# Third stage of a retention and multiplicative-FFN kernel: VectorE's block transposes behind the first work item, v and natural k on ScalarE's DMA queue, unit 10 transposed by TensorE

## The chip, the cores and the metric

The kernel runs on one core of one Trainium2 chip. The metric is the device time of one execution in microseconds (us). The kernel before took 881.2 us, the median of three runs (878.97, 881.2, 881.26); the profiled execution took 879.61, of which the profile's span is 877.6.

Short names used below: PE is TensorE's matmuls, PEld its weight loads, DVE VectorE, ACT ScalarE, POOL GpSimd, and SP SyncE, whose queue issues most of the DMAs. L448 is line 448 of the kernel.

## The reference

The program has two parts. Retention comes first: for 8 sequences, 8 heads, 576 positions and 64 features a head, every score of a query against an earlier key is scaled by a power of a decay, without a softmax, and multiplied with v. The result, 4608 tokens of 512 features, then goes through a multiplicative feed-forward network.

```python
scores = scale * np.matmul(q, k.transpose(0, 1, 3, 2))          # (8, 8, 576, 576)
gamma = 1.0 - 2.0 ** (-5.0 - np.arange(H, dtype=np.float32))
Dmat = np.where(rel >= 0, gamma[:, None, None] ** rel[None], 0.0)
x = np.matmul(scores * Dmat, v)                                 # then to (4608, 512)
a = x @ w1                                                      # (4608, 1024)
b = x @ w2
h = a * b @ w3
return h @ w_out                                                # (4608, 512)
```

The four weight matrices come as 64-bit floats. All else is 32-bit.

## The kernel before

**Units.** The sequences are taken in four pairs i = 0 to 3. The positions of a pair are cut into five chunks c: a short one of 64 positions first, then four of 128. A unit is g = 5i + c, so there are 20 units, and units 5, 10 and 15 are the short first units of the second, third and fourth pair. The decay is split into a factor on q and one on v, so only the triangle of the mask is left inside a chunk.

**The attention work of a unit.**
- `load` (L103) brings q, k or v in natural form, positions on the partitions: one DMA each, 512 KB (256 KB for a short unit).
- `scale` (L203) multiplies q and v by their decay factors on GpSimd.
- `front` (L215) transposes k and q on TensorE, so that the features lie on the partitions, and ScalarE copies them out of PSUM as kT and qT.
- `score` (L232): 32 TensorE matmuls of kT and qT (tile sc, L241), and VectorE multiplies with the triangular mask into pm (L244).
- `state` (L248): k^T v of the chunk is added on TensorE to a running state (L263), and ScalarE copies it to sb for the next unit. The last chunk of a pair has none. It needs k and v in natural form.
- `pv` (L270): TensorE multiplies sb with qT (L291, where there is a chunk before) and pm with v (L298); ScalarE copies the sum into the token tile xT (L303).

**The block form.** For units from 10 on, k and q reach kT and qT without TensorE. `load_blocks` (L168) loads 32x32 blocks with many small DMAs of 32 KB: 16 for k and 16 for q of a full unit, 8 and 8 for a short one, all issued by SyncE. `scale_blocks` (L183) multiplies the blocks of q by the decay in two GpSimd instructions. `front_blocks` (L193) has VectorE transpose every block in one instruction for k and one for q (L198). The natural k is still loaded, for `state`. Tiles of blocks share two buffers with the natural q (tag ld_q), so the loads of one unit wait until the transposes of the unit before have read theirs.

**The feed-forward network.** 192 positions of both sequences of a pair make a token group (i, n), 12 in all. `up(i, n, fp)` (L476) computes a quarter of the products x w1 and x w2 with Strassen's seven products: TensorE multiplies (L493), ScalarE copies the first product (L506, later L513), VectorE adds the others up (L498) and multiplies both halves (L519). `down(x, y)` (L583) does the same for two groups of 128 tokens against the product of w3 and w_out (L599 on TensorE, L603 on VectorE, L621 and L627 on ScalarE) and SyncE stores the result (L644). `carry` is one ScalarE copy (L551). The sums of tokens that Strassen's form needs are made on GpSimd (L467). Seven PSUM buffers (pool acc) serve all of it in rotation.

**The order.** The program is scheduled by hand: each engine does its instructions in the order in which they are written. Three stages follow each other: weights and the first pair, the product of w3 and w_out, and then the third stage, the loop at L805 over the steps g = 5 to 19. There the list `todo` holds the work items, and `work(n)` takes the next n of them. A step does items, then pv(g), then state and score of g + 1, then further items. In steps 10 to 19 there are two items ahead of pv. For the steps that matter, as the code gives them:

| step g | item 1 | item 2 | behind score of g + 1 |
|---|---|---|---|
| 8 | up(1,0,0) | none | none |
| 9 | up(1,0,1) | none | none |
| 10 | up(1,0,2) | up(1,0,3) | up(1,1,0), a down |
| 11 | up(1,1,1) | a down | up(1,1,2) |
| 12 | up(1,1,3) | up(1,2,0) | carry |
| 13 | a down | up(1,2,1) | up(1,2,2) |
| 14 | up(1,2,3) | up(2,0,0) | a down |
| 15 | up(2,0,1) | a down | up(2,0,2), up(2,0,3) |
| 16 | up(2,1,0) | carry | a down, up(2,1,1) |
| 17 | up(2,1,2) | up(2,1,3) | up(2,2,0), a down |
| 18 | up(2,2,1) | a down | up(2,2,2), up(2,2,3) |

Before, the code of a step with blocks (L814 to L829) puts scale_blocks behind item 1 and front_blocks behind item 2, and behind pv(g) SyncE's queue gets the natural v and k of unit g + 2, then its k blocks, then its q blocks.

Of the kernel before, what the change touches and what calls it, by code (L numbers as in the profile page):

```python
# [38 lines left out]
def kernel(  # L39
# [13 lines left out]
    nc = tc.nc  # L53
# [11 lines left out]
    NC = (S + P - 1) // P  # L65
# [3 lines left out]
    G = NB2 * NC  # L69
# [33 lines left out]
    def load(g, names, engine=nc.sync):  # L103
        i, c = divmod(g, NC)
        sz = sizes[c]
        src = {"k": k, "q": q, "v": v}
        for nm in names:
            t = pools["ld"].tile([P, 2 * H, D], F32, tag="ld_" + nm, name="ld_" + nm)
            engine.dma_start(
                t[:sz], src[nm][2 * i:2 * i + 2, :, starts[c]:starts[c] + sz, :].rearrange("b h p d -> p (b h) d"))  # L110
            live[nm, g] = t
# [56 lines left out]
    def load_blocks(g, nm):  # L168

        i, c = divmod(g, NC)  # L170
        n = sizes[c] // BL
        t = pools["ld"].tile([P, 2 * NP, P // BL, BL], F32, tag="ld_q", name="bl_" + nm)
        src = {"k": k, "q": q}[nm][2 * i:2 * i + 2].rearrange("b (p a) s d -> a (b p) s d", a=2)
        for a in range(2):
            for f in range(D // BL):
                part = (a * (D // BL) + f) * BL
                for m in range(n):
                    s0 = starts[c] + m * BL
                    nc.sync.dma_start(t[part:part + BL, :, m, :],  # L179
                                      src[a, :, s0:s0 + BL, f * BL:(f + 1) * BL].rearrange("m r x -> r m x"))  # L180
        live["bl_" + nm, g] = t

    def scale_blocks(g):  # L183
        c = g % NC
        n, n0 = sizes[c] // BL, starts[c] // BL
        t = live["bl_q", g]
        for b in range(2):
            part = t[:, b * NP:(b + 1) * NP, :n, :]
            nc.gpsimd.tensor_tensor(
                out=part, in0=part, in1=gqs[:, :, n0:n0 + n].unsqueeze(3).to_broadcast([P, NP, n, BL]),  # L190
                op=ALU.mult)

    def front_blocks(g):  # L193
        c = g % NC
        n = sizes[c] // BL
        for nm in "kq":
            dst = pools["fr"].tile([P, 2, NP, P], F32, tag=nm + "T", name=nm + "T", bufs=1 if nm == "k" else 2)
            nc.vector.transpose(  # L198
                dst[:, :, :, :sizes[c]].rearrange("p b m (n x) -> p (b m) n x", x=BL),
                live["bl_" + nm, g][:, :, :n, :])  # L200
            live[nm + "T", g] = dst

    def scale(g, nm, scalar=False):  # L203
        c = g % NC
        sz = sizes[c]
        t, gam = live[nm, g], {"q": gq, "v": gk}[nm]
        t = t[:sz].rearrange("p (b h) d -> p b h d", b=2)
        if scalar:
            for h in range(H):
                nc.scalar.mul(t[:, :, h, :], t[:, :, h, :], gam[:sz, c, h:h + 1])  # L210
            return
        nc.gpsimd.tensor_tensor(  # L212
            out=t, in0=t, in1=gam[:sz, c].unsqueeze(1).unsqueeze(3).to_broadcast([sz, 2, H, D]), op=ALU.mult)

    def front(g, names="kq"):  # L215
        c = g % NC
        sz = sizes[c]
        for nm in names:
            src = live[nm, g]
            dst = pools["fr"].tile([P, 2, NP, P], F32, tag=nm + "T", name=nm + "T",  # L220
                                   bufs=1 if nm == "k" and g >= NC else 2)
            for b in range(2):
                tp = acc.tile([P, NP, P], F32, tag="acc", name="tp")
                for p in range(NP):
                    h = b * H + 2 * p
                    nc.tensor.transpose(tp[:, p, :sz],  # L226
                                        src[:sz, h:h + 2, :].rearrange("p a d -> p (a d)"),
                                        ident[:sz, :sz])
                nc.scalar.copy(dst[:, b, :, :sz], tp[:, :, :sz])
            live[nm + "T", g] = dst  # L230
# [39 lines left out]
    def pv(g):  # L270
        i, c = divmod(g, NC)
        sz = sizes[c]
        live["x", g] = True
        qT, vs, pm = live["qT", g], live["v", g], live["pm", g]

        parts = []
        for n in range(NB):
            lo, hi = max(starts[c], n * TB), min(starts[c] + sz, (n + 1) * TB)
            if lo < hi:
                m = i * NB + n  # L280
                if ("xT", m) not in live:
                    live["xT", m] = xps[m % 4 == 3].tile([P, NP, 2, TB], F32, tag="xT", name="xT")
                parts.append((live["xT", m], lo - n * TB, lo - starts[c], hi - lo))

        banks = [acc.tile([P, 2, 2, P], F32, tag="acc", name="xps") for r in range(2)]
        order = [(b, n) for b in range(2) for n in range(2)]
        if c > 0:
            for m, (b, n) in enumerate(order):
                for r, j in ((0, 0), (0, 1), (1, 0), (1, 1)):
                    p = 2 * r + n  # L290
                    nc.tensor.matmul(banks[r][heads[j ^ r], b, n, :sz], live["sb", g][heads[j], b, p, :],  # L291
                                     qT[heads[j], b, p, :sz], start=(m == 0), stop=False,
                                     skip_group_check=True)
        for m, (b, n) in enumerate(order):
            for r in range(2):
                for half in range(2):
                    p, j = 2 * r + n, half ^ r
                    nc.tensor.matmul(banks[r][heads[half], b, n, :sz], vs[:sz, b * H + 2 * p + j, :],  # L298
                                     pm[:sz, b, j, p, :sz], start=(c == 0 and m == 0), stop=True,
                                     skip_group_check=True)  # L300
        for x, to, fr, n in parts:
            for r in range(2):
                nc.scalar.copy(  # L303
                    x[:, 2 * r:2 * r + 2, :, to:to + n].rearrange("p n b s -> p b n s"),
                    banks[r][:, :, :, fr:fr + n])
# [272 lines left out]
    def ahead(x, y, n=3):  # L578
        todo_sums = pair_of(x, y)[2]
        for _ in range(min(n, len(todo_sums))):  # L580
            aside.append(todo_sums.pop(0))
# [203 lines left out]
    def work(n):  # L785
        for _ in range(min(n, len(todo))):
            fn, *args = todo.pop(0)

            nxt = next((x for x in todo if x[0] is not carry), None)
            if nxt and nxt[0] is down and fn is not carry:  # L790
                if fn is down:
                    args.append(nxt[1:])
                else:
                    last = args == [*every[max(nxt[1][0], nxt[2][0])], NQ - 1]
                    ahead(*nxt[1:], 1 if last else 3)
            fn(*args)
# [4 lines left out]
    state(NC)  # L801
    score(NC)
    scale(NC + 1, "q")
    in_blocks = [u >= 2 * NC for u in range(G)] + [False] * 2
    for g in range(NC, G):  # L805
        c = g % NC
        n = -(-len(todo) // (NC - c))
        if g + 2 < G and not in_blocks[g + 2]:
            load(g + 2, "kq")
        if g + 1 < G:  # L810
            scale(g + 1, "v")
            if not in_blocks[g + 1]:
                front(g + 1)
        half = (n + 1) // 2  # L814
        if in_blocks[g + 1]:
            work(1)
            scale_blocks(g + 1)
            work(1)
            front_blocks(g + 1)
            half = max(half - 2, 0)  # L820
        work(half)
        pv(g)
        if g + 2 < G:
            load(g + 2, "v")
        if in_blocks[g + 2]:
            if (g + 2) % NC != NC - 1:
                load(g + 2, "k")
            load_blocks(g + 2, "k")
            load_blocks(g + 2, "q")  # L829
        if g + 1 < G:  # L830
            state(g + 1)
            score(g + 1)
        if g + 2 < G and not in_blocks[g + 2]:
            scale(g + 2, "q")
        if g == NC + 1:
            strassen_tokens(1, 0)
            todo.extend((up, 1, 0, fp) for fp in range(2))
        work(n // 2)
        if c == NC - 1:
            add_pair(g // NC)  # L840
# [44 lines left out]
```

## Time and profile before

| engine | busy us | share of the span |
|---|---|---|
| TensorE, weight loads | 777.6 | 89% |
| GpSimd | 112.2 | 13% |
| DMA from HBM | 53.03 MB | 71 GB/s with the stores |

How to read the rows shown later: in the timeline a row has its start and length in us, the engine, the line, the operation and its tiles (out<-in), then in brackets how long the engine stood idle ahead of it and what ended that wait. In the chain of waits the program is followed back from its end, at each step to what released it. A row of waits gives the total us, how many times, and the longest. Ends of matmuls are modelled, so a wait of a tenth of a us means little.

Some durations in the third stage, as the timeline and the chain have them: an up takes TensorE 9.10 us (9.30 just behind a score), a down 12.09, pv 1.03 and 1.90, a state 0.93, a score of a full unit 1.99. A full k transpose on VectorE takes 1.24 us. GpSimd's scaling of a natural v or q takes 1.90, of a unit's q blocks 2.06. SyncE is held 0.45 us (median) by the issue of one block DMA, which lands about 2 us after it.

### The profile page before, as it was taken

The numbers are of one execution on the slowest core, as the hardware profiler recorded it, in microseconds if no ns is written. First come the engines' busy times: TensorE is split into PE (matmuls) and PEld (weight loads), VectorE is DVE, ScalarE is ACT, GpSimd is POOL, SyncE is SP. The second block draws the span as 40 slices with busy tenths as digits, with TensorE's granted clock in tenths as the row PEclk, the third lists the DMA queues.
The fourth block names the chain that finished last, engine by engine and source line by source line (L and its number), as shares of the span: only waits on it lengthen the run. The fifth ranks groups of instructions, "written<-read, shape, count | busy, mean of one in ns | idle before, by whom it ended". The sixth has DMA issues, their size and how long they took to land.

```text
span 877.6 us, 15316 instructions
## 1 busy us (share of the span) xinstructions
PE 851.1 (97%) x6357; PEld 777.6 (89%) x6357; DVE 458.7 (52%) x783; ACT 193.7 (22%) x386; POOL 112.2 (13%) x92
## 2 busy tenths in 40 slices
PE   5899999999999999899999999999999999999998
PEld 4799999554888999799989998989999999999996
DVE  5999998972544334544444534444534424434243
ACT  3676334553122211101111101110101101001000
POOL 3000020003003201301203012203020101000000
PEclk9999999999999999899999999999999999999999
DMA  9993443427045335513244053251310000000001
GB/s 199 217 229 91 98 121 97 144 96 108 0 100 123 92 49 89 99 32 79 43 70 76 4 105 93 41 88 34 65 33 25 2 24 1 24 25 1 25 1 49
DMA packets 190644, 63.46 MB, mean 72 GB/s; under 512 B 178792, under 2 KB 178792, under 8 KB 190576
## 3 DMA queue, kind: packets, MB, share of 16 engines
q1 hardware_dynamic: 188912, 62.19, 33.5%
q8 instruction: 50, 0.82, 0.4%
q10 hardware_dynamic: 1664, 0.30, 0.3%
q14 instruction: 18, 0.15, 0.1%
HBM read 53.03 MB, written 9.44 MB: 71 GB/s over the span
## 4 chain that ended last, share of the span: by engine, by line
PE 85%; DVE 5%; SPq 2%; issue 2%; DMA 0%; ACT 0%; DVEq 0%; POOL 0%; POOLq 0%; ACTq 0%
PE up L493 44%; PE po L599 24%; PE ps L448 6%; PE sc L241 4%; PE xps L298 3%; SPq L179 2%; PE tp L226 1%; PE xps L291 1%; DVE c L498 1%; PE st L263 1%; DVE qT L198 1%; PE tp L438 1%; DVE kT L198 1%; DVE e L383 0%; DMA bl_q<-in_q_dram 0%
## 5 line engine op out<-in xcount | busy, mean ns | idle before, releaser
L498 DVE TENSOR_TENSOR c<-up,c 128x384 f32<-128x384 f32 x240 | 133.5, 556 | 209.8 <-PE up L493 204.4
L493 PE MATMUL up<-xT,wA 128*128 128x192 f32 x1152 | 213.1, 328 | 0.5 <-ACT xT L303 0.5
L493 PEld LDWEIGHTS up<-xT,wA 128*128 128x128 f32 x1152 | 191.7, 191 | 3.4 <-issue 1.0
L493 PE MATMUL up<-T,wS 128*128 128x192 f32 x768 | 140.6, 326 | 2.1 <-DVE T L467 2.1
L493 PEld LDWEIGHTS up<-T,wS 128*128 128x128 f32 x768 | 127.4, 190 | 2.4 <-issue 2.4
L599 PE MATMUL po<-w3o,ab 128*128 128x256 f32 x456 | 104.2, 380 | 0.2 <-ACT ot L621 0.2
L599 PEld LDWEIGHTS po<-w3o,ab 128*128 128x128 f32 x456 | 85.9, 190 | 12.2 <-ACT ot L621 0.6
L603 DVE TENSOR_TENSOR ot<-po,ot 128x256 f32<-128x256 f32 x90 | 38.2, 424 | 73.5 <-PE po L599 72.9
L513 ACT COPY c<-up 128x384 f32<-128x384 f32 x48 | 22.9, 478 | 226.4 <-PE up L493 222.2
L493 PE MATMUL up<-xT,wS 128*128 128x192 f32 x384 | 70.6, 327 | 0.6 <-DVE c L498 0.5
L493 PE MATMUL up<-T,wA 128*128 128x192 f32 x384 | 70.2, 326 | 0.0
L599 PE MATMUL po<-wB,forms 128*128 128x256 f32 x288 | 65.1, 379 | 0.0
L493 PEld LDWEIGHTS up<-xT,wS 128*128 128x128 f32 x384 | 63.6, 190 | 1.5 <-DVE c L498 1.5
L493 PEld LDWEIGHTS up<-T,wA 128*128 128x128 f32 x384 | 63.7, 190 | 0.0
L244 DVE TENSOR_TENSOR pm<-sc,mask 128x512 f32<-128x512 f32 (+1 forms) x80 | 45.5, 628 | 33.0 <-PE sc L241 33.0
L599 PEld LDWEIGHTS po<-wB,forms 128*128 128x128 f32 x288 | 54.7, 190 | 7.4
L448 PE MATMUL ps<-wo,w3T 128*128 128x512 f32 x128 | 56.4, 593 | 0.2 <-ACT w3T L440 0.2
L212 POOL TENSOR_TENSOR ld_v<-ld_v,gk 128x1024 f32<-128x1024 f32 (+1 forms) x17 | 32.7, 1926 | 155.9 <-DMA ld_v<-in_v_dram 142.9
L506 ACT COPY c<-up 128x384 f32<-128x384 f32 x48 | 22.9, 477 | 132.7 <-PE up L493 84.0
L519 DVE TENSOR_TENSOR ab<-c 128x768 f32<-128x768 f32 x48 | 46.4, 967 | 3.8
L448 PEld LDWEIGHTS ps<-wo,w3T 128*128 128x128 f32 x128 | 23.7, 190 | 27.3 <-issue 26.8
L241 PE MATMUL sc<-qT,kT 64*128 64x128 f32 (+1 forms) x640 | 40.6, 280 | 6.4 <-DVE qT L198 6.4
(75 smaller groups left out, 795.7 us busy)
## 6 DMA issues: line engine op xcount, KB each, us to landing
raw<-in_moe_w_dram SPq DMA_DIRECT2D x24, 512.0 KB, 3.6
ld_v<-in_v_dram SPq DMA_DIRECT2D x16, 512.0 KB, 5.0
ld_k<-in_k_dram SPq DMA_DIRECT2D x14, 512.0 KB, 6.9
out_dram<-ot SPq DMA_DIRECT2D x24, 256.0 KB, 2.0
bl_k<-in_k_dram SPq DMA_DIRECT2D x144, 32.0 KB, 2.2
bl_q<-in_q_dram SPq DMA_DIRECT2D x144, 32.0 KB, 2.0
raw<-in_moe_w_dram SPq DMA_DIRECT2D x16, 256.0 KB, 6.7
ld_q<-in_q_dram SPq DMA_DIRECT2D x8, 512.0 KB, 8.4
```

Source lines behind the costliest of these rows:

```text
L212: nc.gpsimd.tensor_tensor(out=t, in0=t, in1=gam[:sz, c].unsqueeze(1).unsqueeze(3).to_broadcast([sz, 2, H, D]), op=ALU.mult)
L241: nc.tensor.matmul(sc[j][:sz, p, :sz], kT[hs, b, p, :sz], qT[hs, b, p, :sz], start=True, stop=True)
L244: nc.vector.tensor_mul(pm[:sz, b, j, :, :sz], sc[j][:sz, :, :sz], mask[:sz, :sz].unsqueeze(1).to_broadcast([sz, NP, sz]))
L298: nc.tensor.matmul(banks[r][heads[half], b, n, :sz], vs[:sz, b * H + 2 * p + j, :], pm[:sz, b, j, p, :sz], start=(c == 0 and m == 0), stop ...
L448: nc.tensor.matmul(ps, live["w3T", ft][:, g, :], live["wo"][:, g, :], start=(g == 0), stop=(g == KF - 1))
L493: nc.tensor.matmul(ps[:, w, :], a[:, w, r, :], b[:, r, :], start=(new and w == r == 0), stop=(w == r == 1), skip_group_check=True)
L498: nc.vector.tensor_add(c[:, to], ps, c[:, sb])
L506: nc.scalar.copy(c[:, 0], p1)
L513: nc.scalar.copy(c[:, 0], p1)
L519: nc.vector.tensor_mul(ab[:, 4 * fp:4 * fp + 4, :], c[:, :, 0, :], c[:, :, 1, :])
L599: nc.tensor.matmul(ps[nm], a[A][:, f, :], live["W"][B][:, f, :], start=(f == 0 and not on), stop=(f == NP - 1), skip_group_check=True)
L603: nc.vector.tensor_add(ot[:, to[0], to[1]], ps[nm], ot[:, sb[0], sb[1]])
```

## The change

Four things change in the loop of the third stage; the order of the work items stays.

- The transposes of unit g + 1 come behind item 1, not item 2, and the scaling of its q blocks comes ahead of item 1. This is to have kT and qT ready well before score asks for them.
- The block loads of unit g + 2 are issued directly behind those transposes, q before k, and not behind pv(g).
- The natural v and k of a unit in block form are issued from ScalarE's queue, so that SyncE's queue holds only blocks and stores. Their place behind pv(g) stays.
- Unit 10, the short first unit of the third pair, is no longer in block form: its k and q are loaded naturally in step 8, and TensorE transposes them in step 9 (the comparison `u > 2 * NC`). So SyncE can issue unit 11's blocks a step earlier in the run.

```diff
-    in_blocks = [u >= 2 * NC for u in range(G)] + [False] * 2
+    in_blocks = [u > 2 * NC for u in range(G)] + [False] * 2
     for g in range(NC, G):
         c = g % NC
         n = -(-len(todo) // (NC - c))
...
         half = (n + 1) // 2
         if in_blocks[g + 1]:
-            work(1)
             scale_blocks(g + 1)
             work(1)
             front_blocks(g + 1)
-            half = max(half - 2, 0)
+            half = max(half - 1, 0)
+        if in_blocks[g + 2]:
+            load_blocks(g + 2, "q")
+            load_blocks(g + 2, "k")
         work(half)
         pv(g)
+
         if g + 2 < G:
-            load(g + 2, "v")
-        if in_blocks[g + 2]:
-            if (g + 2) % NC != NC - 1:
-                load(g + 2, "k")
-            load_blocks(g + 2, "k")
-            load_blocks(g + 2, "q")
+            queue = nc.scalar if in_blocks[g + 2] else nc.sync
+            load(g + 2, "v", queue)
+            if in_blocks[g + 2] and (g + 2) % NC != NC - 1:
+                load(g + 2, "k", queue)
         if g + 1 < G:
             state(g + 1)
             score(g + 1)
```

## The prediction

> **What bounds the kernel now.** I read the page's busy shares first, then TensorE's own waits, then the stages, then the timeline around each wait.
>
> The busy shares:
> ```profile
> PE 851.1 (97%) x6357; PEld 777.6 (89%) x6357; DVE 458.7 (52%) x783; ACT 193.7 (22%) x386; POOL 112.2 (13%) x92
> ```
> TensorE is busy for 851.1 of 877.6 us; no other engine is near. So an edit can only gain by taking away idle time of TensorE, instructions of TensorE, or time at a low clock. The waits of TensorE in the third stage (215 us to the end), as total, times, longest:
> ```profile
> PE sc L241 <- DVE qT L198: 6.4, 6, 3.9
> PE po L599 <- ACT ot L621: 0.2, 1, 0.2
> ```
> One kind of wait is left there: score (L241) waits for VectorE's transposes of q (L198), six times, 6.4 us. The second row lies at the very end, which the change doesn't touch. The timeline gives the six: 3.92 us at 358.30 (unit 11), 0.22 at 443.08 (unit 13), 1.15 at 470.60 (14), 0.64 at 541.36 (16), 0.23 at 575.00 (17), 0.23 at 620.72 (18): 6.39.
>
> Around the longest, the chain in order of time (start, length, what):
> ```profile
> 352.49 2.17 DMA bl_q<-in_q_dram
> 354.89 0.94 issue
> 355.83 1.06 POOL bl_q L189
> 356.91 1.26 DVE qT L198
> 358.30 3.78 PE sc L241 x32
> 362.09 10.29 PE up L493 x56
> ```
> Unit 11's q blocks land only at 354.7; then come the two POOL scalings, the transpose and the scores. The timeline shows why so late: their DMAs are issued last. The k blocks take SyncE's queue from 333.86 for 11.15 us (behind the natural v and k, and those behind pv(9)), the q blocks from 345.12 for 7.82 us. The stages around it (length, then busy us of PE, PEld, DVE, ACT, POOL, then granted clock, DMA share, GB/s):
> ```profile
> 358.30:360.00 1.70, 1.70 (x16) 1.70 (x18) 0.00 (x0) 0.00 (x0) 1.70 (x3) 0.50 1.13 186
> 360.00:362.00 2.00, 2.00 (x20) 1.79 (x18) 1.29 (x2) 0.00 (x0) 2.00 (x2) 0.50 0.34 48
> 362.00:363.00 1.00, 1.00 (x5) 0.98 (x4) 0.91 (x2) 0.00 (x0) 0.68 (x1) 0.50 0.31 48
> ```
> After this gap TensorE runs at half clock up to 364. The score takes 3.78 us where the others take 2.06, and the next up 10.29 where up(1,0,1) at 319.59, also behind a score, takes 9.30. The shorter waits have no such tail: each of their scores takes 2.06.
>
> They are of another kind:
> ```profile
> 467.21 0.96 DVE L519 TENSOR_TENSOR ab<-c 128x768 f32<-128x768 f32 x1
> ...
> 468.09 1.24 DVE L198 STREAM_TRANSPOSE kT<-bl_k 128x1024 f32<-128x1024 f32 x1
> 469.25 1.20 DVE L198 STREAM_TRANSPOSE qT<-bl_q 128x1024 f32<-128x1024 f32 x1
> ...
> 470.60 2.06 PE L241 MATMUL sc<-qT,kT 64*128 64x128 f32 x32 [1.15 <-DVE qT L198]
> ```
> The blocks of unit 14 are there and scaled by 464.5, but the transposes stand in VectorE's queue behind the last add and the multiply (L519) of item 2, which end only 1.6 us after TensorE has left the item. TensorE has just pv (2.9 us), and a state (0.9) if the unit has one, to cover them.
>
> **What the Trainium skill says.** "TensorE: Matmul & The Clock Gate", Part 1: an idle window of about 3.4 us puts the clock to half, and about as long a busy one brings it back. The trace agrees: after 3.92 us idle 0.50 is granted up to 364; after 1.15 us it isn't. "DMA: Bandwidth & Descriptors", Issuing engines are not separate DMA queues: queues of two engines share the same DMA engines, and a second queue saves only sequencer time. "Perfetto Trace Analysis", DMA Instruction — HWDGE: a DMA's bar is the time in which its sequencer is held, not the movement of data. Before, one natural load was issued by ScalarE, at 0.80 us, and held it 0.75 us; in this stage there is none.
>
> **The change, part by part.**
>
> (1) Transposes one item earlier (units 11 to 19). VectorE's queue becomes: adds of item 1, kT, qT (1.24 + 1.14, since they overlap), adds of item 2. They end about 1.6 + 2.4 = 4.0 us after TensorE began item 2, some 11 us before the score needs them (9.1 or 12.1 of item 2, 2.9 of pv, less 4.0). All six waits but one go: in step 16 item 2 is a carry, a ScalarE copy with no TensorE work, so unit 17 keeps its 0.23. Gain 6.39 - 0.23 = 6.16 us. What is queued behind the transposes: item 2's adds, and TensorE needs these. In an up the first add is ready at about 2.8 us and now starts at 4.0; adds of 0.56 us come 1.30 apart, so VectorE has caught up by the fourth. TensorE needs the third when it accumulates S4 into p5, 7.8 us into the item; three adds end by 6.0. The seven PSUM buffers last until then. Cost nothing, with 1.8 us to spare: that is how late the transposes may be.
>
> (2) q and k blocks earlier, q first. They are issued once the transposes of the unit before have freed the tiles, not behind pv and the natural loads. 32 issues take some 16 to 18 us (7.8 to 9.1 per 16). The shortest way from transposes to transposes is step 12 to 13: with item 1 of step 12 ending at X, loads go from X+4 to X+21, land 2.2 us later (X+25 with a v load between); VectorE is at unit 14's transposes at X + 9.1 + 2.9 + 0.9 + 2.1 + 12.1 + 0.7 = X+27.8. 3 us remain. Unit 11's blocks are now issued in step 9, from about 318; q lands at about 330, k at about 339, item 1 of step 10 ends near 344. So the 3.92 wait goes, counted in (1), and with it the half clock: (3.78 - 2.06) + (10.29 - 9.30) = 2.71 us.
>
> (3) v and natural k on ScalarE. They are issued behind the xT copies of pv, so their wait for pv costs nothing. Holding time, from SyncE's rows: v 0.39, k behind it 0.67 to 2.87. I take 2.1 (0.39 + 1.69, as at 353.34); the upper bound is two loads each held like the block DMA behind a k, 3.45: 6.9. Behind them stand the copy of sb (0.59, wanted a step later) and the first copy of the next item. Counted from the end of pv: copies 1.0, loads 2.1, sb 0.6, so 3.7. An up begins at 3.0 and accumulates into p1 at 9.5; a down begins at 3.0 and accumulates into its first bank at 6.6. Nothing is lost at 2.1; at 6.9 the down that follows in step 14 loses about 2.3, the ups nothing.
>
> (4) Unit 10 by TensorE. Gone: 16 block DMAs, 2.0 us of POOL, two transposes of 0.70. Added on TensorE: 16 transposes, which the chain shows for unit 5, of the same 64 rows: 1.14 us for the sixteen. This is on the path: +1.14. Four ScalarE copies (1.3 us), a POOL scaling of q (1.9) and the natural q load, issued at about 302, lie beside up(1,0,0), long before they are needed at 319.6.
>
> (5) Scaling of blocks ahead of item 1: POOL reaches it sooner and the token sums (four of 1.0 us) come behind it. The blocks have landed by then, so 2.06 us hidden beside an up.
>
> Sum: -6.16 - 2.71 + 1.14 = -7.73. 881.2 - 7.7 = 873.5 us.
>
> **The rivals.**
>
> *Part of it comes back.* The natural loads move beside the k blocks; v or k lands late (natural loads took 4.2 to 12.3 us), POOL scales late, and VectorE, now in front of item 2's adds, sits in the transposes. Tightest are steps 10 and 13. With 2 to 5 us of stalls in all: 875.5 to 878.5, say 876.5. For: DMA share was 0.6 to 0.8 where both kinds ran. Against: 3 us of slack each.
>
> *A new wait takes the gain.* The same, in steps 10, 12 and 13, and each over 2 us, or a fresh gap over 3.4 us with its half clock (2.7): 7 to 8 us, 881.
>
> *Slower: ScalarE is held.* The loads on its queue start while SyncE is still issuing k blocks. If each waits for several of these, 10 us for a pair, the first copies are late: an up loses 2.6 us (1.0 + 10 + 0.6 + 0.5 = 12.1 against 9.5), a down 5.4 (12.0 against 6.6). Five ups (steps 9, 10, 11, 13, 15) and the down of step 14 give 18 us: 892. Steps 12 and 17 load v alone; step 16 issues its loads before its blocks. For: a DMA behind a natural k took 3.45 us. Against: SyncE's block issues are 0.45 us each, and at 0.80 us both queues issued together, 0.75 each.
>
> **How the numbers follow.** Forecast 0.71, part of it back 0.18, gain taken 0.06, slower 0.05. Faster by over 0.3% (2.6 us, below 878.6): 0.71 + nearly all of 0.18 = 0.88; same 0.06; slower 0.06. Range: below, the three times differ by 2.3 us (878.97 to 881.26), so 870.5; above, the second case up to 877.5.
>
> **What would show it.** Right: no row of score waiting for qT but unit 17's; unit 11's score 2.06 us, no 0.50 clock in the stage; sixteen 64-row transposes just behind unit 9's score; loads on ScalarE's queue of some 2 us a pair. Wrong: TensorE waiting in ups for VectorE's adds (transposes late), in a down for ScalarE's ot copy (loads held), VectorE idle for block DMAs ahead of kT, or a lowered clock elsewhere.

## The result, and the profile after

The changed kernel takes 872.67 us (median; 872.37 to 874.54), the kernel before 881.0 beside it. The ratio is 0.9915, 95% interval [0.9895, 0.9935]. A second set on another occasion gave 872.82 us and 0.9911 [0.9898, 0.9925]. The forecast was 873.5 us, within 870.5 to 877.5.

The busy shares of the page after:
```profile
PE 851.9 (98%) x6373; PEld 779.0 (89%) x6373; DVE 458.3 (53%) x781; ACT 194.7 (22%) x390; POOL 111.8 (13%) x91
```
TensorE is busy about as long as before (851.1 us) in a span that is 6.9 us shorter. The equality is an accident of the first stages. From up(1,0,0) on, TensorE is busy for 559.75 us after and 561.83 before: the 16 added transposes of unit 10 are in it, and the half clock that had stretched some matmuls is gone. Ahead of that it is busy for 292.12 us after and 289.26 before, where the change does nothing; this execution happened to run at half clock from 34.9 to 38.4 us there, and that of the kernel before didn't.

TensorE's waits in the third stage after (total, times, longest):
```profile
PE po L599 <- ACT ot L621: 0.3, 1, 0.3
PE sc L241 <- DVE qT L198: 0.2, 1, 0.2
```
Of the 6.4 us in which score waited for qT, 0.2 is left. It is at 568.23: unit 17, whose step has a carry as its item 2. The other row is the end of the kernel, as before.

The chain of work around unit 11 after (start, length, what):
```profile
335.99 18.40 PE up L493 x112
354.39 1.08 PE xps L298 x32
355.46 1.08 PE st L263 x32
356.55 1.99 PE sc L241 x32
358.53 9.30 PE up L493 x56
```
DMA, POOL and VectorE are gone from it: up, up, pv (the row xps), state (st), score (sc) and up follow each other on TensorE. The score takes 1.99 us where it took 3.78, the up behind it 9.30 where it took 10.29. The granted clock is 1.00 here.

VectorE and TensorE in step 10 after, as the timeline has them:
```profile
345.12 1.46 PE L493 MATMUL up<-xT,wA 128*128 128x192 f32 x8
...
345.99 0.96 DVE L519 TENSOR_TENSOR ab<-c 128x768 f32<-128x768 f32 x1
...
346.86 1.24 DVE L198 STREAM_TRANSPOSE kT<-bl_k 128x1024 f32<-128x1024 f32 x1
...
348.02 1.20 DVE L198 STREAM_TRANSPOSE qT<-bl_q 128x1024 f32<-128x1024 f32 x1
...
349.15 1.18 DVE L498 TENSOR_TENSOR c<-up,c 128x384 f32<-128x384 f32 x2
...
350.52 0.56 DVE L498 TENSOR_TENSOR c<-up,c 128x384 f32<-128x384 f32 x1 [0.20 <-PE up L493]
...
352.92 1.46 PE L493 MATMUL up<-xT,wS 128*128 128x192 f32 x8
```
Item 2 begins at 345.12. The transposes end at 349.22, two late adds follow without a gap, and at the third VectorE already waits for TensorE again (0.20 us). TensorE wants the third add at 352.92, and it ends at 351.08.

Counting from the start of up(1,0,0) to the end of the span leaves out the first two stages, whose length differs by a us or two from one execution to the next. Before: 877.6 - 305.57 = 572.0 us. After: 870.7 - 306.75 = 564.0 us. The difference is 8.1 us. By the chains of the two traces it is made of unit 10's transposes, +0.98; unit 11's wait, -3.99, its score, -1.73 (against the 2.05 that other scores behind a wait take), and the up behind it, -0.99; the short waits of units 13, 14, 16 and 18, -0.19, -1.12, -0.63 and -0.19; and some -0.2 of matmuls that now follow without a break.

### The profile page after: what moved, and what is told of

The parts are those of the page before. It is cut to its first block, busy times and chain, and to the rows that moved or that the text cites. A ratio compares the mean times of both kernels' runs of the same rounds, so it can differ in the third digit from the quotient of the medians.

```text
span 870.7 us, 15305 instructions
## 1 busy us (share of the span) xinstructions
PE 851.9 (98%) x6373; PEld 779.0 (89%) x6373; DVE 458.3 (53%) x781; ACT 194.7 (22%) x390; POOL 111.8 (13%) x91
## 4 chain that ended last, share of the span: by engine, by line
PE 88%; DVE 3%; issue 1%; DMA 1%; ACT 1%; DVEq 0%; ACTq 0%; SPq 0%
PE up L493 46%; PE po L599 25%; PE ps L448 6%; PE sc L241 4%; PE xps L298 3%; PE xps L291 2%; PE tp L226 1%; PE st L263 1%; DVE c L498 1%; PE tp L438 1%; DVE e L383 0%; DMA raw<-in_moe_w_dram 0%; ACT e L372 0%; DVE ab L519 0%; DVE w L392 0%
## 5 line engine op out<-in xcount | busy, mean ns | idle before, releaser
L467 POOL TENSOR_TENSOR T<-xT,T 128x384 f32<-128x384 f32 x20 | 20.9, 1043 | 217.1 <-PE up L493 215.4
```

## The experiments

My theory was that two different causes share one row of waits. Unit 11's q came late by DMA, and is cured by issuing its blocks a step earlier, which only unit 10's conversion allows. The short waits come from the place of the transposes in VectorE's queue. The rivals: one of the edits does it all; the ScalarE queue matters; the transposes are hidden by luck. Two parts of the change were never undone alone, the order q before k and the scaling ahead of item 1, and the place of the block loads only together with that of the transposes.

Where kernels differ by a us or two, a second count helps: from the start of the third stage's first down to the end of the span, in the profiled execution. That down starts anywhere from 230.5 to 232.5 us, for reasons that lie ahead of every edit. The count is 647.1 us before (877.6 - 230.49), and 639.0 and 639.1 in the two traces of the changed kernel.

**Unit 10 alone.**
```diff
 # the kernel before
-    in_blocks = [u >= 2 * NC for u in range(G)] + [False] * 2
+    in_blocks = [u > 2 * NC for u in range(G)] + [False] * 2
```


> The kernel before with unit 10 transposed by TensorE, and nothing else of the change. My theory: unit 11's blocks are still issued behind pv(9) and the natural loads, so its q still lands near 355, the score of unit 11 still waits about 3.9 us and runs at half clock, and TensorE has 1.0 us more to do: 882.0 us, 1.0 above before. Rival (converting unit 10 alone frees SyncE's queue early enough): the wait and its half clock go, 875.4 us.

Measured: 881.62 us, ratio 1.001 [0.9997, 1.0022]. That is 1.2 us above the 880.41 beside it, though the interval still holds 1; the second count, 648.3 us, is 1.2 above before too. Its timeline:
```profile
361.13 3.44 PE L241 MATMUL sc<-qT,kT 64*128 64x128 f32 x32 [5.37 <-DVE qT L198]
```
The long wait stays, and in this trace it is longer (5.37 us for 3.92), and the short ones keep their lengths. The conversion alone gains nothing.

**The transposes alone.**
```diff
 # the kernel before
-            work(1)
             scale_blocks(g + 1)
             work(1)
             front_blocks(g + 1)
-            half = max(half - 2, 0)
+            half = max(half - 1, 0)
```


> The kernel before with only the transposes moved behind item 1 and the scaling of q blocks ahead of it; loads, queues and unit 10 as before. My theory: the short waits go (-2.2 us), but where the blocks land late VectorE now sits in the transposes in front of item 2's adds. Step 10: q of unit 11 lands at 354.7, transposes end at 358.2, three adds later TensorE goes on at 360 where it wanted p5 at 350.7: 9 us and a half clock of 2.7 in place of 6.6. Step 13: the same with about 4 us and a half clock. 892 us (887 to 896), slower than before. Rival (the place of the transposes is what gains, the loads hardly matter): 873 to 876 us.

Measured: 896.39 us, 1.0177 [1.0156, 1.0197], 16 us slower than before. TensorE's waits in the third stage:
```profile
PE up L493 <- DVE c L498: 11.2, 2, 8.7
PE up L493 <- POOL T L467: 4.4, 1, 4.4
PE sc L241 <- DVE qT L198: 0.2, 1, 0.2
```
The score no longer waits; the ups do. In step 10:
```profile
358.70 1.25 DVE L198 STREAM_TRANSPOSE qT<-bl_q 128x1024 f32<-128x1024 f32 x1 [8.57 <-POOL bl_q L189]
...
359.87 2.51 DVE L498 TENSOR_TENSOR c<-up,c 128x384 f32<-128x384 f32 x4
...
361.77 2.93 PE L493 MATMUL up<-xT,wS 128*128 128x192 f32 x8 [8.74 <-DVE c L498]
```
VectorE stands 8.57 us in front of a transpose with four adds behind it, and TensorE stops for 8.74 (expected 9). In step 13 it is 2.50 us (expected 4). I had not expected the second row. The scaling of q blocks moves ahead of item 1 with this edit, so where blocks are late GpSimd waits for them with the token sums behind it, and an up waits 4.38 us for its tokens. Waits of 15.8 us against 6.4 before make 9.5 of the 16 us. The rest is half clock: in the third stage 20.4 us of it here and 6.8 before, so 13.6 more, of which about half is lost.

**The changed kernel with unit 10 in blocks.**
```diff
 # the changed kernel
-    in_blocks = [u > 2 * NC for u in range(G)] + [False] * 2
+    in_blocks = [u >= 2 * NC for u in range(G)] + [False] * 2
```


> The changed kernel with unit 10 back in block form. My theory: unit 11's blocks can be issued only behind unit 10's transposes (about 333), q and k take till 350 or, if the natural loads hold the block stream up by 5 us, till 355, and VectorE sits in front of up(1,0,3)'s adds; TensorE wants the third at 352 and gets it at 355 to 360: 3 to 8 us and a half clock of 2.7, less the 1.0 us of TensorE transposes saved: 877.5 to 882.5, I say 881. So TensorE's transposes of unit 10 carry most of the gain of unit 11. Rival (the earlier place of the loads is enough without it): 871.7 us.

Measured: 879.6 us, 0.999 [0.9977, 1.0002]: the gain is gone.
```profile
354.69 1.25 DVE L198 STREAM_TRANSPOSE kT<-bl_k 128x1024 f32<-128x1024 f32 x1 [8.18 <-DMA bl_k<-in_k_dram]
...
358.88 2.93 PE L493 MATMUL up<-xT,wS 128*128 128x192 f32 x8 [6.22 <-DVE c L498]
```
Unit 11's blocks are issued only from 332.93, behind unit 10's transposes. This is the one wait that comes back. So unit 10's TensorE transposes cost about 1.0 us of TensorE time and, with the rest of the change in place, are worth 7. The profiled run was at the long end: the twelve timed runs go from 878.70 to 882.69, most near 879.5. In the profiled one the half clock behind the gap lasted 10.2 us; whether it was shorter in the others is not known, so why some runs take 3 us more stays open.

**The changed kernel with the transposes late.**
```diff
 # the changed kernel
             work(1)
-            front_blocks(g + 1)
             half = max(half - 1, 0)
+        work(half)
+        if in_blocks[g + 1]:
+            front_blocks(g + 1)
         if in_blocks[g + 2]:
             load_blocks(g + 2, "q")
             load_blocks(g + 2, "k")
-        work(half)
         pv(g)
```


> The changed kernel with the transposes, and so the block loads behind them, put back behind item 2; unit 10 by TensorE, q before k, and v and k on ScalarE stay. My theory: the short waits return (0.22, 1.15, 0.64, 0.23 for units 13, 14, 16, 18) and unit 11 gets one of the short kind (0.6), the long one does not: 2.9 us more than the changed kernel, 875.6 us. Rival (the whole gain lies in the loads): 872.7 us. Other rival (loads an item later are late again): 878 us and more, with a half clock in the trace.

Measured: 878.03 us, 0.9972 [0.9962, 0.9981], so 5.2 to 5.4 us above the changed kernel and not 2.9. Its waits of TensorE:
```profile
PE sc L241 <- DVE qT L198: 4.4, 6, 1.9
PE po L599 <- ACT ot L621: 1.3, 2, 1.0
```
4.4 + 1.0, less the 0.2 that the changed kernel has too, are the 5.2. The four short waits are back at their old lengths. The time is that of the other rival, loads that come late again (878 and more), but its sign is missing: there is no half clock in the third stage, and the last k block of unit 11 was issued by 343.0 us, where VectorE reached its transpose only at 356.21. Two sizes were off in my sum. Unit 11's wait is 1.92. I had taken the kind of unit 16 (0.64), whose item 2 is a down; behind an up VectorE ends its transposes 4.0 us after TensorE has left the item, and pv and state cover only 2.16 of that. The other us is a wait for ScalarE in the down of step 14:
```profile
506.11 0.38 ACTq L109 DMA_DIRECT2D ld_k<-in_k_dram  x1
506.52 0.58 ACT L267 COPY sb<-st 128x512 f32<-128x512 f32 x1 [4.83 <-DMA bl_q<-in_q_dram]
507.00 0.38 ACT L621 COPY ot<-po 128x256 f32<-128x256 f32 x1
...
507.43 1.78 PE L599 MATMUL po<-w3o,ab 128*128 128x256 f32 x7 [0.99 <-ACT ot L621]
```
With the blocks issued just ahead of the natural loads, k on ScalarE's queue waited until a block DMA had landed, and held ScalarE 4.83 us. This is the prediction's rival of a held ScalarE, at 1 us where that rival had 18.

**v and natural k on SyncE again.**
```diff
 # the changed kernel
-            queue = nc.scalar if in_blocks[g + 2] else nc.sync
+            queue = nc.sync
```


> The changed kernel with v and natural k issued from SyncE's queue again, behind the blocks. My theory: the ScalarE queue is worth nothing here; v of unit 14, the tightest, comes about 7 us later and still in time, and the block stream is no longer held up by natural loads on another queue: 872.7 us, within 1 us of the changed kernel, no new wait of TensorE. Rival (natural loads behind 16 to 18 us of block issues arrive late): POOL scales v late, q's transpose behind it, a wait of some us in steps 10 and 13: 875 us and more.

Measured: 873.29 us, 0.9916 [0.9904, 0.9929], the same as the changed kernel; the second count is 639.1 us. No wait of TensorE is added. Unit 11's k blocks on SyncE, first in the changed kernel and then in this one:
```profile
327.69 15.21 SPq L179 DMA_DIRECT2D bl_k<-in_k_dram  x16
```
```profile
328.51 8.92 SPq L179 DMA_DIRECT2D bl_k<-in_k_dram  x16
```
The second queue makes the block stream slower, not faster, and neither is on the path. What it does buy is margin for q: GpSimd has scaled unit 14's q blocks by 446.7 in the changed kernel, 7.5 us before VectorE transposes them, and by 454.3 here, 0.7 us before.

**Every transpose twice.**
```diff
 # the changed kernel, in front_blocks
-            nc.vector.transpose(...)
+            for _ in range(2):
+                nc.vector.transpose(...)
```


> The changed kernel with every transpose of blocks done twice into the same tile: 2.4 us more on VectorE in eight steps and 1.4 in step 14. My theory (hidden beside item 2 with 1.8 us to spare): transposes end 6.5 us into item 2, three adds end near 8.3, wanted at 7.8: 0.5 us lost in the four steps where item 2 is an up and the unit is full (10, 12, 13, 17), none where it is a down or the unit is short, and the full 2.4 in step 16, whose item 2 is the carry: 4.4 us more, 877.1 us. Rival (transposes are on the path): 9 steps of 1.4 to 2.4, 20 us more, 893 us. Other rival (slack is larger than I think): only step 16, 875.1 us.

Measured: 879.43 us, 0.999 [0.9982, 0.9999]: 6.7 us above the changed kernel, not 4.4 and not 20. The line numbers are higher by one in this kernel.
```profile
352.85 1.57 PE L494 MATMUL up<-xT,wS 128*128 128x192 f32 x8 [0.52 <-DVE c L499]
...
434.50 1.57 PE L494 MATMUL up<-xT,wS 128*128 128x192 f32 x8 [1.32 <-DVE c L499]
...
572.41 3.69 PE L242 MATMUL sc<-qT,kT 64*128 64x128 f32 x32 [2.78 <-DVE qT L199]
...
614.90 1.57 PE L494 MATMUL up<-xT,wS 128*128 128x192 f32 x8 [0.52 <-DVE c L499]
```
Steps 10 and 17 lose the 0.5 us that the slack said. Step 12 loses 1.32: between the adds of its up, VectorE also makes three sums for the next down, 0.67 us each, so it catches up later there. Step 13 loses nothing: its item 1 is a down, behind which VectorE is free a us sooner. Step 16 pays the doubling in full, and its 2.78 us of idling is followed by half clock (the score takes 3.69 for 2.06). Together 0.52 + 1.32 + 0.52 + 2.78 + 1.63, less the 0.22 that step 16 waits anyway, are 6.6.

**Fewer TensorE transposes.** If block loads early enough hide all, units of steps with one item can have the block form too.
```diff
 # the changed kernel
-    in_blocks = [u > 2 * NC for u in range(G)] + [False] * 2
+    in_blocks = [u in (9,) or u > 2 * NC for u in range(G)] + [False] * 2
...
+        early = in_blocks[g + 1] and n == 1
+        if early:
+            scale_blocks(g + 1)
+            front_blocks(g + 1)
         if g + 2 < G and not in_blocks[g + 2]:
             load(g + 2, "kq")
...
-        if in_blocks[g + 1]:
+        if in_blocks[g + 1] and not early:
             scale_blocks(g + 1)
```


> The changed kernel with unit 9, too, in block form: its blocks are loaded in step 7 and transposed by VectorE at the start of step 8, ahead of its only item. TensorE is spared 16 full transposes, 1.90 us. My theory: the blocks land about when step 8 starts, VectorE's slack of 1.8 us in up(1,0,0) takes the rest: 870.8 us. Rival (a step with one item, 18 us, is too short for 32 block loads): VectorE sits in front of the adds, TensorE loses the 1.9 us again or more: 872.7 to 876 us.

Measured: 871.36 us, 0.9898 [0.9885, 0.9911]. The interval overlaps with the changed kernel's, so the times alone don't separate the two. The second count does it better: 637.5 us, 1.5 below the changed kernel, and no wait of TensorE is added. With `(7, 9)` in place of `(9,)`:

> As the kernel before this one in the list, with unit 7 in block form as well, loaded in step 5 and transposed at the start of step 6. My theory: another 1.90 us saved, 868.9 us. Rival (block loads of 16 to 18 us do not fit the 18 us of steps 5 and 7): 872.7 to 878 us.

Measured: 874.43 us, 0.9936 [0.9923, 0.9948], slower than unit 9 alone. The rival is right on the time. The cause is not VectorE standing in front of its adds, but a store:
```profile
267.00 1.74 SPq L644 DMA_DIRECT2D out_dram<-ot  x3
...
271.16 0.37 ACT L621 COPY ot<-po 128x256 f32<-128x256 f32 x1 [7.47 <-DMA out_dram<-ot]
...
271.58 3.47 PE L599 MATMUL po<-w3o,ab 128*128 128x256 f32 x8 [3.65 <-ACT ot L621]
```
Step 5's result is stored only at 267.00, when SyncE is through with unit 7's blocks. There is one ot tile, and the next down, in step 6, waits for it: 3.65 us and a half clock. Of the delay, 4.9 us is the second queue's doing: SyncE stood from 260.7 to 265.6 for the natural v that ScalarE issued at 261.35, with three of unit 7's blocks and this store still to come. So by an estimate from these times, v on SyncE behind the store might have done too; no run tried it. Instead, the stores go to ScalarE's queue:
```diff
 # the kernel with units 7 and 9 in blocks, in store()
-            nc.sync.dma_start(*stores.pop(0))
+            nc.scalar.dma_start(*stores.pop(0))
```


> The kernel with units 7 and 9 in block form, and its stores issued from ScalarE's queue and not SyncE's. There, the down of step 6 waited 3.65 us for its ot tile, whose store stood on SyncE's queue behind unit 7's blocks, and ran its next matmuls at half clock. My theory (that store is the whole trouble): wait and half clock go, and the store issues hold ScalarE for no longer than its slack: 869.3 us, 1.9 below the kernel with unit 9 alone in block form (871.4). Rival (a store waits on ScalarE's in-order queue for VectorE's last add, with the copies of the next item behind it): TensorE waits for ScalarE in the ups behind downs, 872 us and more.

> The changed kernel itself, beside the run before it in this list, for a direct comparison on one chip: 872.7 us, ratio 0.991 to before.

Measured side by side: 869.46 us, 0.9886 [0.9864, 0.9908], and the changed kernel 872.82, 0.9911 [0.9898, 0.9925]. TensorE's waits of the former:
```profile
PE sc L241 <- ACT qT L229: 0.4, 1, 0.4
PE up L493 <- DVE c L498: 0.3, 1, 0.3
PE po L599 <- ACT ot L621: 0.3, 1, 0.3
PE sc L241 <- DVE qT L198: 0.2, 1, 0.2
```
The 3.65 is gone, and the 0.4 and 0.3 are what is new. The two intervals overlap by 0.001; four of its five runs (869.31 to 869.99) lie below all five of the changed kernel (871.57 and more), one (873.73) doesn't. It has the lowest median of the study, 3.4 us below the changed kernel. Part of this may not be the edit's: four of its five runs were granted a mean clock of 1.000, four of the changed kernel's 0.998, a difference as large as one half clock of 3.4 us makes. By the second count, 636.6 us, it is 2.4 us below.

## Why the prediction was right, and where its working was off

From up(1,0,0) on, the traces differ by 8.1 us where the sum said 7.7.

(1) *Transposes one item earlier: right.* Forecast: the transposes end 4.0 us into item 2, the third add at 6.0, wanted at 7.8; in step 10 they are 4.1, 5.96 and 7.80. Forecast gain of the short waits 2.24 us; by the chains 2.13, and the late-transposes run gives the waits back at their old lengths. The slack of 1.8 us is the size that the doubled transposes bear out (0.52 where 0.5 was worked out), except where an up also makes a down's sums: there it is about 1.1 (2.4 more, 1.32 lost).

(2) *Blocks earlier: right in what it removes, off in when k lands.* The wait and half clock were put at 3.92 and 2.71; the chains give 3.99 and 2.72. But k of unit 11 was to land at about 339, with 16 to 18 us for 32 issues. SyncE was stopped for 5.2 us in the middle of them, the last six are issued from 338.68 for 4.22 us, and with 2.2 us to landing k is there at about 345, 2 us ahead of VectorE and not 7. The working had SyncE's queue free once the natural loads left it. TensorE saw none of this, but that is luck in part: the margin held, though not for the reason given.

(3) *v and k on ScalarE: right, and worth nothing.* A v held ScalarE for 0.38 us (median) and a k for 1.63, 2.0 together where I took 2.1. No first copy came late. What a longer hold does shows only in the late-transposes run, where one of 5.6 us (500.92 to 506.49) cost 0.99; by the working a down has 4.5 us of slack, which fits.

(4) *Unit 10 by TensorE: about as charged,* 0.98 us by the chain for 1.14. From the first transpose to the next matmul's start it is 1.08 us for unit 10 (320.61 to 321.69) and 1.13 for unit 5 (242.67 to 243.80), so most of the difference lies in modelled ends. The forecast charged it as a cost with the gain of unit 11 under another heading. The runs show that the two belong together: about 1 us lost when made alone, 7 us lost if taken back out.

(5) *Scaling ahead of item 1: no wait for it in the trace, as forecast, since the blocks are early.* With late blocks, in the transposes-alone run, TensorE waited 4.38 us for tokens behind it.

Of the rivals, that of part coming back was wrong for this change, since no VectorE wait for blocks appears in the trace. Its mechanism is real all the same: the transposes-alone run is just that case, 16 us slower. The rival of ScalarE being held was shown only at 1 us, with another order of the loads.

## What to carry to other kernels

Moving an operation ahead in an in-order queue helps only once what it waits for is early too; otherwise it takes everything behind it along: the transposes ahead of item 2 save about 4 us of score waits with early loads (so much comes back in the late-transposes run) and cost 16 us without. An edit that only costs when made alone can be what frees the queue or buffer for all the others, so edits of a bundle have to be undone one by one as well as done one by one. When a queue gets a long stream of loads, look for what else stands in it, and for what can stop it: here a store behind unit 7's blocks cost more than moving that unit's transposes off TensorE saved.

## What the runs showed of the hardware and the program that I had not expected

Loads on a second queue held up the first. In the trace every DMA that SyncE and ScalarE issue signals its landing on one of the same eight semaphores (counters on which engines wait), and an issue that is to use one waits until the earlier DMA on it has landed. The k block that SyncE issues at 338.68 uses the semaphore of the natural v that ScalarE issued at 334.11 and that landed at 338.66. SyncE's waits in the changed kernel, 300 to 700 us:
```profile
SPq L179 <- DMA ld_v<-in_v_dram: 29.7, 7, 5.9
```
Seven times the block stream stood still for a natural v, 29.7 us in all; with v and k on SyncE this row is absent, and the issue of unit 11's k blocks takes 8.92 us for 15.21. The 4.83 us on ScalarE in the late-transposes run is the same thing the other way round: k has the semaphore of a q block issued at 500.52, which landed at 506.08.

The clock fell after shorter gaps than "TensorE: Matmul & The Clock Gate" says in Part 1 (about 3.4 us). In the third stage it fell after 2.50 us (transposes alone, 481.24: 2.35 us for matmuls that otherwise take 1.46 to 1.57) and after 2.78 us (transposes twice), and not after 1.92. In the first stage all twelve traces have the same gap of 2.08 to 2.09 us, at about 33; the clock fell behind it in seven of them (at 34.9 in the changed kernel's first trace) and not in the other five, the trace of before and the changed kernel's second among them. So by these runs a gap of 2.1 us is already at risk, and whether it costs anything varies between executions of one kernel.

Each fall lasted 3.4 us, or two or three times that: 3.4 after gaps of 2.50, 2.78, 3.65 and 5.37 us, 6.8 after 3.92 and 4.38, 10.2 after 6.22 and 8.74. At half speed up to half of it is lost, so 1.7, 3.4 or 5.1 us on top of the gap. In the kernel before, TensorE stayed at half clock until 364.1, 5.8 us after it had resumed at 358.30, which is longer than the busy stretch of about 3.4 us that the prediction reckoned with.
